# A written order for VectorE, ScalarE, GpSimd and the loads up to the second product, in a fused retention and SiLU kernel

## The chip, the cores and the metric

The kernel runs on one core of a Trainium2 chip. TensorE (PE in the profile; PEld is its weight load) multiplies into PSUM, VectorE (DVE) and ScalarE (ACT) work elementwise, GpSimd (POOL) makes constants, and SyncE (SP) issues DMAs between HBM and SBUF. The metric is the device time of one execution in microseconds (us), as a median over runs; lower is better.

## The reference

Two parts follow each other. Retention: for 4 batches and 8 heads, over 768 positions with head size 64, a 64x64 state decays and takes up the outer product of k and v, and q reads it. Then a feed-forward part on the 3072 x 512 result.

```python
gamma = 1.0 - 2.0 ** (-5.0 - np.arange(H))
for t in range(S):
    state = gamma[None, :, None, None] * state + np.einsum('bhd,bhe->bhde', k[:, :, t], v[:, :, t])
    y[:, :, t] = scale * np.einsum('bhd,bhde->bhe', q[:, :, t], state)
x = y.transpose(0, 2, 1, 3).reshape(B * S, H * D)
h = x @ w_in                      # 512 -> 2048
g = h * (1.0 / (1.0 + np.exp(-h)))
out = g @ w_out                   # 2048 -> 512
```

q, k and v are 32-bit floats. `w_in` and `w_out` arrive as 64-bit floats and are converted on the chip. All three products are made at about 32-bit accuracy, each from three products of rounded parts.

## The kernel before

**Units.** The sequence is cut into 6 chunks of 128 positions; a chunk of one batch is a *unit*, 24 in all, 0 to 3 being chunk 0 of the four batches, 4 to 7 chunk 1, and so on. A unit loads k, q and v (256 KB each, `load`, L137). The units go through a pipeline of *visits* (`halves`, L544): visit m transposes k and q of unit m (`stage_t`, L396; ScalarE copies them out, L405), makes the sums and scores of unit m-1 (`stage_s` L419, `stage_a` L429) and y of unit m-2 (`stage_y`, L462). VectorE scales k (`scale_k`, L365), masks the scores (am, L437), forms mid and state (L446, L450; mid is a ScalarE copy in chunk 0, L444), scales q (L370) and splits y into three parts of x (`finish_y`, `split_x`: ScalarE L497 and L509, VectorE L512 and L513). From unit 6 on, ScalarE scales k, a head at a time (L354). Between two parts of a unit's y stands a fence, a tiny GpSimd memset (L340).

**Slices of the weights.** `w_in` is used in 16 slices of 128 columns. A slice's 64-bit words are loaded by three DMAs (`load_w`, L170 and L172, 512 KB), converted by one ScalarE operation and six of VectorE (`convert_w`, L198 to L215), and split into three parts by two ScalarE and two VectorE operations (`split_w`, L121 to L126). `take_w` does a whole slice; `begin_w` and `end_w` do it in two visits.

**Products.** `product_in(c, f)` (L592) multiplies chunk c's x by slice f: 8 matmuls into bank ha, 4 into hb (L596). The first four need the rounded high parts, the next four the second parts, and hb the third ones. ScalarE copies ha out (L600), VectorE subtracts hb (L604), ScalarE applies SiLU (L608), and `put_g` stores g to HBM. Product (c, f) needs all four units of chunk c and slice f. The products of chunks 0 to 2 run among the visits; those of later chunks follow. After all g is stored, chunk by chunk, g is loaded back, split (L651 to L654) and multiplied by `w_out` (L761) into pairs of accumulators oa and ob for four batches, which are evacuated (L769 and L770; in the last chunk L773 and L778) and stored.

**What sets the order.** TensorE's order is the program's (`manual_schedule`, L663). That of the other engines and of SP's queue is chosen by the framework's scheduler when the kernel is built; the kernel steers it only with `issue_after`, which puts instructions behind a given one of the same engine. On a queue or engine an instruction that waits holds up what is behind it. Before TensorE's schedule starts, all loads of units 0 to 7 are issued, with slice 0 after unit 1 and slice 1 after unit 4:

```python
    for n in range(EARLY):            # EARLY = 8
        for name in "kqv":
            load(name, n)
        if n in (1, 4):
            load_w(n // 4)
```

The visits then run as follows: product (0, 0) after visit 6, (0, 1) after visit 8, (0, 2) in the middle of visit 9, and (1, 0) after the first half of visit 10.

```python
    for m in range(EARLY + 1):
        visit(m)
        if m == 2:
            take_w()
        elif m == EARLY - 2:
            product_in(0, 0)
            load_w(3)
        elif m == EARLY:
            product_in(0, 1)
            put_g(1)
```

Of the kernel before, what the change touches and what calls it, by code (L numbers as in the profile page):

```python
# [15 lines left out]
U32 = mybir.dt.uint32  # L16
# [17 lines left out]
def kernel(  # L34
# [79 lines left out]
    def split_w(f, w32, name, factor, to, behind_x=False):  # L114


        to[f] = w = w_slot(f, name)
        lo = conv.tile([128, 512], FP32, tag="wl", name=f"{name}l_{f}")
        yield
        with tc.issue_after(held[0] if behind_x or f >= NF - 4 else evac[0]):  # L120
            nc.scalar.activation(out=w[:, 0, :], in_=w32, func=AF.Copy, scale=HALF * factor)  # L121
        high = w[:, 0, :].bitcast(FP32)
        nc.vector.scalar_tensor_tensor(out=lo, in0=w32, scalar=factor, in1=high,
                                       op0=ALU.mult, op1=ALU.subtract)
        nc.scalar.activation(out=w[:, 1, :], in_=lo, func=AF.Copy, scale=1.0 / EPS)
        nc.vector.scalar_tensor_tensor(out=w[:, 2, :], in0=high, scalar=EPS, in1=lo,  # L126
                                       op0=ALU.mult, op1=ALU.subtract)

# [48 lines left out]
    def convert_w(i):  # L177

        if i + W_AHEAD not in staged and i != 1:
            load_w(i + W_AHEAD)
        t = staged.pop(i)
        if not wide:  # L190
            return lambda: t
        words = t.rearrange("p (c w) -> p c w", w=2)
        lo, hi = words[:, :, 0], words[:, :, 1]
        a = conv.tile([128, DM], U32, tag="ca", name=f"ca_{i}")
        s = conv.tile([128, DM], U32, tag="cs", name=f"cs_{i}")
        p = conv.tile([128, DM], U32, tag="cp", name=f"cp_{i}")
        with tc.issue_after(evac[0]) if evac else ExitStack():
            nc.scalar.activation(out=a.bitcast(FP32), in_=hi.bitcast(FP32), func=AF.Abs,  # L198
                                 scale=65536.0)
        nc.vector.tensor_scalar(out=s, in0=hi, scalar1=0x80000000, scalar2=None,  # L200
                                op0=ALU.bitwise_and)
        nc.vector.tensor_scalar(out=a.bitcast(FP32), in0=a.bitcast(FP32),
                                scalar1=bits(1024 << 20), scalar2=bits((1279 << 20) - 1),
                                op0=ALU.max, op1=ALU.min)
        nc.vector.scalar_tensor_tensor(out=s, in0=a, scalar=3, in1=s,  # L205
                                       op0=ALU.logical_shift_left, op1=ALU.bitwise_or)
        nc.vector.tensor_scalar(out=p, in0=s, scalar1=0xFF800000, scalar2=None,
                                op0=ALU.bitwise_and)
        nc.vector.scalar_tensor_tensor(out=p.bitcast(FP32), in0=lo, scalar=2.0 ** -52,  # L209
                                       in1=p.bitcast(FP32), op0=ALU.mult, op1=ALU.mult)  # L210

        def rounded():
            w = (s.bitcast(FP32) if i < NF else
                 conv.tile([128, DM], FP32, tag="wl", name=f"cw_{i}"))
            nc.vector.tensor_tensor(out=w, in0=s.bitcast(FP32), in1=p.bitcast(FP32), op=ALU.add)  # L215
            return w

        return rounded

# [39 lines left out]
    for n in range(EARLY):  # L259
        for name in "kqv":  # L260
            load(name, n)
        if n in (1, 4):
            load_w(n // 4)
# [24 lines left out]
    def chunk_decays():  # L288
        pos = step[:, HP + H :]
        nc.gpsimd.iota(pos, pattern=[[0, 1]], base=1, channel_multiplier=1,  # L290
                       allow_small_or_imprecise_dtypes=True)
        for h in range(H):
            nc.scalar.activation(out=gk[:, 0, h : h + 1], in_=pos, func=AF.Exp,
                                 scale=float(-lg[h]))
            nc.gpsimd.memset(step[:, HP + h : HP + h + 1], math.exp(-C * lg[h]))
            part = ts(h % 2, D)
            nc.gpsimd.memset(step[part, h // 2 : h // 2 + 1], math.exp(C * lg[h]))
            nc.gpsimd.memset(lgc[part, h // 2 : h // 2 + 1], lg[h])
        for c in range(1, NC):
            nc.gpsimd.tensor_tensor(out=gk[:, c, :], in0=gk[:, c - 1, :],  # L300
                                    in1=step[:, HP : HP + H], op=ALU.mult)

    def first_chunk():
        nc.gpsimd.iota(lag, pattern=[[1, C]], base=1, channel_multiplier=0,
                       allow_small_or_imprecise_dtypes=True)
        for a in range(HP):
            nc.scalar.activation(out=gq[:, a, :], in_=lag, func=AF.Exp, scale=lgc[:, a : a + 1])

        nc.scalar.activation(out=token, in_=lgc[:1, :1], func=AF.Silu)
# [123 lines left out]
    def finish_a(n, sc, sums):  # L433

        c, b = units[n]
        am[n] = one.tile([128, 2, HP, D], FP32, tag="am", name=f"am_{n}")
        mask = nc.vector.tensor_tensor(out=am[n], in0=sc, in1=decay, op=ALU.mult).ins  # L437
        masked[:] = [mask]
        mid = one.tile([128, HP, D], FP32, tag="mid", name=f"mid_{n}", bufs=2)
        steps_of[n] = state.get(b), mid  # L440

        with tc.issue_after(mask):
            if c == 0:
                nc.scalar.copy(out=mid, in_=sums[:, 0])  # L444
            else:
                nc.vector.tensor_tensor(out=mid, in0=state[b], in1=sums[:, 0], op=ALU.add)  # L446
            if c < NC - 1:
                state[b] = one.tile([128, HP, D], FP32, tag="state", name=f"state_{n}",
                                    bufs=B + 2)
                nc.vector.tensor_tensor(out=state[b], in0=mid, in1=sums[:, 1], op=ALU.add)  # L450
# [37 lines left out]
    def finish_y(n, yp):  # L488
        c, b = units[n]
        if b == 0:  # L490
            p, tag = (wpool, "wq") if c == LATE else (xpool, "xt")
            xt[c] = p.tile([128, 3, KIN, NT], FP32R, tag=tag, name=f"xt_{c}")
        raw = None
        if c <= LATE:

            raw = hpool.tile([128, KIN, C], FP32, tag="hs", name=f"ys_{n}")
            nc.scalar.copy(out=raw.rearrange("p a (o t) -> p o a t", o=2), in_=yp)  # L497
            if c == LATE:
                nc.sync.dma_start(out=y_dram[b], in_=raw)
        split_x(c, b, yp, raw)  # L500

    def split_x(c, b, y, raw):
        x = [xt[c][:, i, :, ts(b, C)] for i in range(3)]
# [7 lines left out]
        def rest():  # L511
            nc.vector.tensor_tensor(out=xl, in0=src, in1=xh.bitcast(FP32), op=ALU.subtract)  # L512
            nc.vector.scalar_tensor_tensor(out=x[2], in0=x[1].bitcast(FP32),  # L513
                                           scalar=-1.0 / EPS, in1=x[0].bitcast(FP32),
                                           op0=ALU.mult, op1=ALU.add)


        if c > LATE or c == LATE and y is not None:
            behind_next.append(rest)
        else:  # L520
            rest()


# [10 lines left out]
    def late_x(b):  # L534
        if b == 0:
            xt[LATE] = xpool.tile([128, 3, KIN, NT], FP32R, tag="xt", name=f"xt_{LATE}")
        with tc.issue_after(copied[0]), tc.issue_after(taken_out[0]):
            split_x(LATE, b, None, y_late.pop(b))
# [5 lines left out]
    def halves(m):  # L544
# [22 lines left out]
        if m == 0:  # L567
            chunk_decays()
            first_chunk()
# [13 lines left out]
        if EARLY - 3 <= m < 3 * B + 2:  # L583
            with tc.issue_after(masked[0]):
                end_w()
                if m not in (EARLY - 2, EARLY):
# [5 lines left out]
    def product_in(c, f):  # L592
        ha, hb = turn(f"ha_{c}_{f}"), turn(f"hb_{c}_{f}")
        for i in range(3):
            for kk in range(KIN):
                nc.tensor.matmul(hb if i == 2 else ha, lhsT=w_sb[f][:, i, ts(kk, 128)],  # L596
                                 rhs=xt[c][:, i, kk, :], start=kk == 0 and i != 1,
                                 stop=kk == KIN - 1 and i != 0)
        hs = hpool.tile([128, NT], FP32, tag="hs", name=f"g_{c}_{f}")
# [63 lines left out]
    ctx.enter_context(tc.manual_schedule(engines={mybir.EngineType.PE}))  # L663


    for m in range(EARLY + 1):
        visit(m)
        if m == 2:
            take_w()
        elif m == EARLY - 2:  # L670
            product_in(0, 0)
            load_w(3)
        elif m == EARLY:
            product_in(0, 1)
            put_g(1)
    half_visits = (x for m in range(EARLY + 1, 3 * B + 1) for x in chain(halves(m), (None,)))
    next(half_visits)
    product_in(0, 2)
    put_g(1)
    next(half_visits)  # L680
# [58 lines left out]
    for c in range(NC):  # L739
        acc = []  # L740
        for b in range(B):
# [3 lines left out]
            else:  # L745
                acc.append([turn(f"oa{b}_{c}"), turn(f"ob{b}_{c}") if b == 2 else
                            banks("q", f"ob{b}_{c}", 1)[:, 0]])
        for f in range(NF):
# [4 lines left out]
            t = ready.pop(n)  # L753
            first_, last = f == 0, f == NF - 1
            for b in range(B):
                gh, glo, gm = (t[:, i, ts(b, C)] for i in range(3))
                oa, ob = acc[b]
                todo = [(oa, gh, 0), (oa, glo, 1), (ob, gm, 2)]

                for o, g, i in todo if c < NC - 1 else todo[2:] + todo[:2]:  # L760
                    nc.tensor.matmul(o, lhsT=g, rhs=wo[f][:, i, :], start=first_ and i != 1,  # L761
                                     stop=last and i != 0)
# [49 lines left out]
```

## Time and profile before

| what | value |
|---|---|
| median of 4 runs | 629.75 us (628.37 to 631.83) |
| the profiled execution's own time | 629.2 us |
| its span, from first to last instruction of the program | 627.4 us |
| mean granted TensorE clock | 0.996 |
| start of product (0, 0) / (0, 1) / (0, 2) / (1, 0) | 37.02 / 50.65 / 55.33 / 61.56 us |
| first work of VectorE | 7.86 us |
| landing of slice 0 / slice 1 / slice 2 | 12.2 / 26.3 / 41.2 us |
| landing of q of unit 7 / unit 8 | 36.6 / 42.8 us |
| first and last matmul of the second matrix product | 359.7 and 622.4 us |

The profile is one execution. Its page gives busy times by engine, 40 slices of the span, DMA queues, the chain of work that ended last, and the costliest groups of instructions. A line of a timeline reads: start, duration, engine, source line, operation, output<-inputs, shape, and in brackets how long the engine had been idle and what ended that. "Issue" means that the engine waited for nothing that the profile shows.

### The profile page before, as it was taken

To read this page: it belongs to the slowest core of one execution; us is meant where nothing else is said; L and a number is where in the kernel's file an instruction comes from. 1 tells how busy PE (TensorE), PEld (TensorE's weight loads), DVE (VectorE), ACT (ScalarE), POOL (GpSimd) and SP (SyncE) were. 2 spreads that over 40 slices of the span, in tenths; PEclk is the share of its full clock that TensorE was granted. 3 is DMA by queue.
4 is the path that set the end of the run, shared out by engine and by line. 5 is a ranking of instruction groups with operands and counts; after the bars stand their busy time and mean duration, and the time that the engine had idled before them with its cause. 6 is when DMAs were issued, how large, how long until landed. Compare 5 with 4: busy or idle time off the path is not lost.

```text
span 627.4 us, 13502 instructions
## 1 busy us (share of the span) xinstructions
PE 603.6 (96%) x5384; PEld 497.0 (79%) x5384; DVE 422.2 (67%) x729; ACT 318.9 (51%) x611; POOL 22.3 (4%) x79
## 2 busy tenths in 40 slices
PE   4778999999999999999999999999999999999997
PEld 3667787888888888888787888888788888888785
DVE  2887998698979876867598795644636453644631
ACT  5688897667665566666466871412222221412211
POOL 3000000000000311111000000000000000000000
PEclk9999999999999999999999999999999999999999
DMA  9987887445559899989566673432523433433301
GB/s 199 212 202 193 214 227 227 160 158 172 202 168 251 208 268 229 262 216 290 195 223 198 217 218 118 140 129 71 178 88 116 154 101 100 142 127 105 97 1 67
DMA packets 137999, 107.32 MB, mean 171 GB/s; under 512 B 94800, under 2 KB 103248, under 8 KB 137936
## 3 DMA queue, kind: packets, MB, share of 16 engines
q1 hardware_dynamic: 135056, 101.21, 57.3%
q10 hardware_dynamic: 2880, 5.24, 2.3%
q8 instruction: 42, 0.69, 0.5%
q14 instruction: 21, 0.17, 0.1%
HBM read 66.06 MB, written 36.70 MB: 164 GB/s over the span
## 4 chain that ended last, share of the span: by engine, by line
PE 88%; DVE 4%; DMA 3%; issue 2%; SPq 2%; ACT 1%; DVEq 0%; ACTq 0%; POOLq 0%
PE ha L596 26%; PE o L761 21%; PE oa L761 14%; PE hb L596 13%; PE ob L761 7%; PE y L462 4%; PE sc L419 2%; PE sc L429 2%; SPq L150 1%; PE qp L403 1%; PE kp L403 1%; DMA kqv<-in_q_dram 1%; DMA wf<-in_moe_w_out_dram 1%; DMA gr<-gd 1%; DMA gd<-g 1%
## 5 line engine op out<-in xcount | busy, mean ns | idle before, releaser
L596 PE MATMUL ha<-xt,wi 128*128 128x512 f32 x768 | 193.1, 393 | 0.8 <-DVE g L604 0.8
L596 PEld LDWEIGHTS ha<-xt,wi 128*128 128x128 f32 x768 | 142.1, 188 | 32.3 <-DVE g L604 2.0
L761 PE MATMUL o<-wo,gs 128*128 128x512 f32 x576 | 146.3, 389 | 0.0
L761 PEld LDWEIGHTS o<-wo,gs 128*128 128x128 f32 x576 | 108.1, 188 | 22.5
L653 DVE TENSOR_TENSOR gs<-gr,gs 128x512 fp32r<-128x512 f32 x96 | 62.3, 685 | 85.3 <-ACT gs L651 85.3
L651 ACT ACTIVATE gs<-gr 128x512 fp32r<-128x512 f32 x96 | 53.5, 621 | 127.9 <-issue 123.6
L761 PE MATMUL oa<-wo,gs 128*128 128x512 f32 x384 | 118.4, 389 | 0.0
L596 PE MATMUL hb<-xt,wi 128*128 128x512 f32 x384 | 103.0, 390 | 0.2 <-ACT g L600 0.2
L604 DVE TENSOR_TENSOR g<-g,hb 128x512 f32<-128x512 f32 x96 | 65.6, 683 | 47.2 <-ACT g L600 34.3
L596 PEld LDWEIGHTS hb<-xt,wi 128*128 128x128 f32 x384 | 71.8, 188 | 16.0 <-ACT g L600 1.2
L761 PEld LDWEIGHTS oa<-wo,gs 128*128 128x128 f32 x384 | 72.0, 188 | 15.3 <-ACT o L769 0.3
L608 ACT ACTIVATE g<-g 128x512 f32<-128x512 f32 x96 | 60.5, 631 | 44.0 <-DVE g L604 43.9
L761 PE MATMUL ob<-wo,gs 128*128 128x512 f32 x192 | 75.3, 392 | 0.3 <-DVE o L770 0.3
L600 ACT ACTIVATE g<-ha 128x512 f32<-128x512 f32 x96 | 56.9, 592 | 29.2 <-PE ha L596 20.2
L654 DVE SCALAR_TENSOR_TENSOR gs<-gs 128x512 fp32r<-128x512 f32 x96 | 62.2, 684 | 0.1
L761 PEld LDWEIGHTS ob<-wo,gs 128*128 128x128 f32 x192 | 36.0, 188 | 9.4 <-DVE o L770 2.1
L198 ACT ACTIVATE ca<-wf 128x512 f32<-128x512 f32 x32 | 21.6, 674 | 10.1 <-DVE cs L205 5.8
L209 DVE SCALAR_TENSOR_TENSOR cp<-wf,cp 128x512 f32<-128x512 uint32 x32 | 22.7, 711 | 0.6
L769 ACT ACTIVATE o<-o 128x512 f32<-128x512 f32 x10 | 6.0, 600 | 33.4 <-PE o L761 33.0
L205 DVE SCALAR_TENSOR_TENSOR cs<-ca,cs 128x512 uint32<-128x512 uint32 x32 | 22.1, 690 | 0.8
L462 PE MATMUL y<-qt,mid 64*64 64x64 f32 x384 | 20.4, 221 | 0.0
L770 DVE TENSOR_TENSOR o<-o,o 128x512 f32<-128x512 f32 x10 | 6.8, 688 | 19.3 <-ACT o L769 19.3
(85 smaller groups left out, 566.9 us busy)
## 6 DMA issues: line engine op xcount, KB each, us to landing
gd<-g SPq DMA_DIRECT2D x96, 256.0 KB, 3.3
gr<-gd SPq DMA_DIRECT2D x96, 256.0 KB, 2.7
wf<-in_moe_w_out_dram SPq DMA_DIRECT2D x16, 512.0 KB, 4.3
out_dram<-o ACTq DMA_DIRECT2D x20, 256.0 KB, 2.1
wf<-in_moe_w_in_dram SPq DMA_DIRECT2D x16, 256.0 KB, 4.2
wf<-in_moe_w_in_dram SPq DMA_DIRECT2D x32, 128.0 KB, 4.0
kf<-in_k_dram SPq DMA_DIRECT2D x16, 256.0 KB, 5.3
qf<-in_q_dram SPq DMA_DIRECT2D x16, 256.0 KB, 4.4
```

Source lines behind the costliest of these rows:

```text
L198: nc.scalar.activation(out=a.bitcast(FP32), in_=hi.bitcast(FP32), func=AF.Abs, scale=65536.0)
L205: nc.vector.scalar_tensor_tensor(out=s, in0=a, scalar=3, in1=s, op0=ALU.logical_shift_left, op1=ALU.bitwise_or)
L209: nc.vector.scalar_tensor_tensor(out=p.bitcast(FP32), in0=lo, scalar=2.0 ** -52, in1=p.bitcast(FP32), op0=ALU.mult, op1=ALU.mult)
L462: i = nc.tensor.matmul(yp[ts(e, D), o, a, :], lhsT=lhsT, rhs=rhs, start=(e, o) not in started, stop=True, skip_group_check=True).ins
L596: nc.tensor.matmul(hb if i == 2 else ha, lhsT=w_sb[f][:, i, ts(kk, 128)], rhs=xt[c][:, i, kk, :], start=kk == 0 and i != 1, stop=kk == KIN ...
L600: copied[:] = [nc.scalar.activation(out=hs, in_=ha, func=AF.Copy, scale=ONE_E).ins]
L604: taken_out[:] = [nc.vector.tensor_tensor(out=hs, in0=hs, in1=hb, op=ALU.subtract).ins]
L608: nc.scalar.activation(out=hs, in_=hs, func=AF.Silu)
L651: nc.scalar.activation(out=t[:, 0, :], in_=g, func=AF.Copy, scale=HALF)
L653: nc.vector.tensor_tensor(out=t[:, 1, :], in0=g, in1=high, op=ALU.subtract)
L654: nc.vector.scalar_tensor_tensor(out=t[:, 2, :], in0=t[:, 1, :].bitcast(FP32), scalar=-1.0 / EPS, in1=high, op0=ALU.mult, op1=ALU.add)
L761: nc.tensor.matmul(o, lhsT=g, rhs=wo[f][:, i, :], start=first_ and i != 1, stop=last and i != 0)
```

## The change

Up to the second product the order of VectorE, ScalarE, GpSimd and SP is written down as well. The helpers become generators whose steps are single instructions (`convert_steps`, `split_steps`, `steps_a`, `steps_y`), and a list of calls puts them in order: T transposes a unit, K scales its k, SC makes sums and scores, A is one step of am, mid and state, Q scales q, YA and YB are the two parts of y, X one step of copying out and splitting y, W one step of a slice.

- Loads: units 0 to 5 are issued at the start, slice 0 after unit 0, slice 1 after unit 3; then slice 2, units 6 and 7, slice 3.
- Product (0, 0) stands after the transposes of unit 4 and (0, 1) after those of unit 5, then visits 6 and 7, (0, 2) in the middle of visit 8, visit 9 and the first half of visit 10. From product (1, 0) on, TensorE's order is as before.
- Slices 2 and 3 begin in visits 6 and 8 (before: 7 and 9).
- The constants are made in a written order; the memsets of `step` come after what the first unit needs.
- A conversion keeps ca and cp in one buffer, and `w_out`'s converted slices have a buffer of their own.
- In the second matrix product every chunk takes oa before ob in a step (the last chunk began with ob). In the last chunk the last two steps are taken batch by batch: ob for both, then oa for both, so that the batches finish one after the other.

```diff
-    for n in range(EARLY):
+    ctx.enter_context(tc.manual_schedule(engines={mybir.EngineType.PE}))
+    early_order = ExitStack()
+    early_order.enter_context(tc.manual_schedule(engines={
+        mybir.EngineType.SP, mybir.EngineType.DVE, mybir.EngineType.Activation,
+        mybir.EngineType.Pool}))
+    for n in range(EARLY - 2):
         for name in "kqv":
             load(name, n)
-        if n in (1, 4):
-            load_w(n // 4)
+        if n in (0, 3):
+            load_w(n // 3)
...
-        a = conv.tile([128, DM], U32, tag="ca", name=f"ca_{i}")
+        p = a = conv.tile([128, DM], U32, tag="ca", name=f"ca_{i}")
...
+    def early_slice(i):
+        out = []
+        yield from convert_steps(i, out)
+        yield
+        steps = split_steps(i, out[0], "wi", scale, w_sb, None)
+        next(steps)
+        yield from steps
...
-        if EARLY - 3 <= m < 3 * B + 2:
+        if EARLY - 2 <= m < 3 * B + 2:
             with tc.issue_after(masked[0]):
                 end_w()
-                if m not in (EARLY - 2, EARLY):
+                if m not in (EARLY - 1, EARLY + 1):
                     begin_w()
...
+    T(0), K(0)
+    nc.scalar.activation(out=token, in_=lgc[:1, :1], func=AF.Silu)
+    SC(0), A(0), Q(0), A(0), A(0)
+    W(0), W(0), W(0), W(0), W(0)
+    YA(0), YB(0), X(0)
+    T(1), K(1)
+    W(0)
+    load_w(2)
+    W(0)
+    X(0), X(0)
+    SC(1), A(1)
...
+    YA(3), YB(3), X(3), X(3)
+    W(1)
+    T(4), K(4)
+    X(3), X(3)
+    W(1), W(1), W(1)
+    loads(EARLY - 2), loads(EARLY - 1)
+    first_of = multiply(0, 0)
+    next_chunk()
+    SC(4)
+    close_in(0, 0, *first_of)
+    put_g(1)
+    W(1)
+    A(4)
+    W(1), W(1)
+    A(4), A(4), Q(4)
+    W(1), W(1)
+    T(5), K(5)
+    taken[0] = 2
+    load_w(3)
+    early_order.close()
+
+    product_in(0, 1)
+    put_g(1)
+    visit(EARLY - 2)
+    visit(EARLY - 1)
+    eighth = halves(EARLY)
+    next(eighth)
     product_in(0, 2)
     put_g(1)
-    next(half_visits)
+    list(eighth)
+    visit(EARLY + 1)
+    half_visits = (x for m in range(EARLY + 2, 3 * B + 1) for x in chain(halves(m), (None,)))
     next(half_visits)
...
-                todo = [(oa, gh, 0), (oa, glo, 1), (ob, gm, 2)]
-
-                for o, g, i in todo if c < NC - 1 else todo[2:] + todo[:2]:
+                for o, g, i in (oa, gh, 0), (oa, glo, 1), (ob, gm, 2):
...
+        for b in range(B if early_f < NF else 0):
+            oa, ob = acc[b]
+            for o, parts in (ob, (2,)), (oa, (0, 1)):
+                for f in range(early_f, NF):
+                    for i in parts:
+                        nc.tensor.matmul(o, lhsT=ready[c * NF + f][:, i, ts(b, C)],
+                                         rhs=wo[f][:, i, :], start=False,
+                                         stop=f == NF - 1 and i != 0)
```

## The prediction

> **What bounds the kernel now.** I read the totals first (the second line is a DMA queue: packets, MB, share), then the table of windows, then the timeline of the first 65 us, and last the chain of waits at the end. The totals:
>
> ```profile
> PE 603.6 (96%) x5384; PEld 497.0 (79%) x5384; DVE 422.2 (67%) x729; ACT 318.9 (51%) x611; POOL 22.3 (4%) x79
> ...
> q8 instruction: 42, 0.69, 0.5%
> ```
>
> TensorE (PE) is idle for 627.4 - 603.6 = 23.8 us of the span. The change adds no matmul and removes none, so it can only move these 23.8 us. The windows say where they lie (columns: PE, PEld, DVE, ACT, POOL busy, granted clock, DMA share, GB/s):
>
> ```profile
> 0.00:10.00 10.00, 4.19 (x16) 2.86 (x16) 1.42 (x2) 6.74 (x24) 4.83 (x41) 1.00 0.95 183
> 10.00:20.00 10.00, 7.62 (x194) 6.50 (x192) 5.25 (x11) 4.15 (x9) 0.16 (x2) 0.83 1.24 215
> 20.00:30.00 10.00, 7.31 (x263) 6.43 (x264) 9.75 (x20) 7.76 (x17) 0.18 (x2) 1.00 0.96 224
> 30.00:40.00 10.00, 7.98 (x239) 7.00 (x239) 8.56 (x17) 7.76 (x21) 0.29 (x2) 1.00 0.88 199
> 40.00:50.00 10.00, 6.21 (x270) 5.43 (x268) 9.15 (x19) 8.93 (x26) 0.43 (x2) 1.00 0.82 187
> 50.00:60.00 10.00, 9.61 (x167) 7.93 (x168) 6.65 (x12) 8.20 (x20) 0.09 (x1) 1.00 0.69 184
> 60.00:70.00 10.00, 9.56 (x160) 7.58 (x159) 9.30 (x20) 8.10 (x21) 0.09 (x1) 1.00 0.84 196
> 70.00:80.00 10.00, 10.00 (x177) 8.21 (x178) 9.60 (x19) 8.94 (x24) 0.09 (x1) 1.00 0.96 249
> 90.00:100.00 10.00, 9.38 (x99) 7.32 (x92) 9.93 (x20) 9.02 (x23) 0.00 (x0) 1.00 0.88 238
> ```
>
> In the first 50 us PE is idle for 5.8 + 2.4 + 2.7 + 2.0 + 3.8 = 16.7 us; from 50 to 100 us for 1.5 us; the end after the last matmul has most of the rest. So the head is what the change can win. But there VectorE (DVE) is busy for 27.5 of the 30 us from 20 to 50 and stays above 9.3 of 10 to 100 us, and the DMA share is 0.82 or more. Three resources are near their limit together. What the idle stretches wait for:
>
> ```profile
> 30.77 0.35 PE L462 MATMUL y<-am,kqv 64*64 64x64 f32 x9 [1.59 <-issue]
> ...
> 35.37 0.27 PE L462 MATMUL y<-am,kqv 64*64 64x64 f32 x2 [1.25 <-issue]
> ...
> 45.85 0.44 PE L403 MATMUL qp<-ident,qf 128*128 128x128 f32 x2 [2.10 <-issue]
> ...
> 50.39 0.27 PE L462 MATMUL y<-qt,state 64*64 64x64 f32 x1 [2.07 <-issue]
> ...
> 58.57 0.69 DVE L604 TENSOR_TENSOR g<-g,hb 128x512 f32<-128x512 f32 x1 [3.11 <-ACT g L600]
> ```
>
> Four times PE waits for nothing in the program, 7.0 us together. Counted along PE's and PEld's records these places are numbers 961, 1217, 1729 and 1985: always a multiple of 256 apart. The totals agree: 5384 + 5384 instructions over 42 fetches is 256 each. So PE is waiting for its own instructions: the resumption at 30.77 is 5.1 us after the one at 25.68 (number 705), 35.37 is 4.6 later, 50.39 is 4.5 after 45.85. I take 4.8 us for every 256 PE instructions while the DMA is this full.
>
> **The change, part by part.** *Constants.* GpSimd's selects now stand ahead of the memsets, so `decay` need not wait for 4.01 and gk is ready near 4.4. The first scaling of k (7.86 before, released by gk) then follows its transpose's end at 5.43: 5.5. What this is worth is part of the walk below.
>
> *Loads.* Slice 0 goes ahead of unit 1, slice 1 ahead of unit 4, slice 2 ahead of unit 6. Before, the DMAs of a unit land 1.2 us apart, a slice's three take 1.03 + 0.56 + 0.49. So slice 0 lands at 6.60 + 2.1 = 8.7 (12.2 before), unit 1's v at 12.2 (10.1), unit 3's v stays at 20.4 and slice 1 lands near 22.5 (26.3). Queued behind them on SP: units 6 and 7 by about 37 and 40, slice 3, the first store of g, and only then k and q of unit 8, after 9.17 MB instead of 8.39.
>
> *VectorE's order, walked.* Ready 512-wide operations start 0.60 apart, 256-wide ones 0.33, dependent ones 0.71. am of unit 0 starts at 8.4 (sums after v at 6.6, then scores 0.75), w0's add at 13.3, am of unit 1 at 14.5, w0's last split at 17.8, am of unit 2 at 18.35, of unit 3 at 22.2, k of unit 4 at 26.2, then the last two x pieces: 28.2. Product (0,0) starts at about 26.2 (37.0 before) and ends at 29.5. Then eleven VectorE operations for g, slice 1 and unit 4 end w1's last split at 34.6; product (0,1) ends at 35.7 (53.7 before).
>
> This is 18 us earlier, and hardly any of it is a gain: by then PE has done some 1150 instructions (16 for a unit's transposes, 128 for its scores, 96 or 128 for its y, 24 for a product), where the records before count 2017. The orders meet again at product (1,0), 61.56 before, whose hb part at 63.51 needs the last x piece of unit 7. What VectorE does from 35.1 to there: one g (0.6), four units' am, mid, q, state (7.5), four x pairs (4.8), slice 2 (4.2), slice 3 up to its first split (3.6), another g (0.6) = 21.3, where 0.5 more goes to dependent steps. Its idle: 0.6 for product (0,1)'s end; 2.55 while PE does unit 6's transposes, y of unit 4 and the scores of unit 5; 0.85 behind ScalarE's thirteen operations (k of unit 6 alone costs 2.02, as before); 1.55 because product (0,2) waits for slice 2's last split and the next am stands behind it; 0.35 for the scores of unit 7: 5.9. The sum is 35.1 + 21.3 + 0.5 + 5.9 = 62.8, against 63.51: **-0.7**. The cause is that slice 3 now converts ahead of (1,0), 3.0 us of work that was partly behind it. I take -0.55, as ends are later by pipeline latency.
>
> PE's fetch pace allows no more than 2.9 us: number 1217 falls in y of unit 4 at 37.4, four more blocks give 56.6 for number 2241, the rest to (1,0) and its ha part bring hb to 60.6.
>
> In the Trainium skill, "Runtime: NRT & Kernel Launch", section "Instruction fetch mechanics", instruction memory is refilled in blocks of 256 instructions and the cost of crossing a boundary is called mostly hidden. The block size agrees with the rows here, the hiding does not (1.25 to 2.10 us each). By the page the 7.0 us would be removable by order alone and the sum below would be that much lower; by the rows they are a pace, and I go by the rows.
>
> *After (1,0).* PE has no gap to 96.8, so VectorE's lead (1.2 us of slice 3's splits plus about 1.7) buys only the waits of PE for VectorE at 97.44 (0.62) and 100.78 (0.17): between 0 and -0.8; **-0.4**, the middle, as DMA stores also stand in that chain.
>
> *Own buffers of the conversions.* One buffer serves ca and cp, another cw: a later slice's first step waits for the earlier one's add. Takes are at least two products (5.4 us) apart, which hides it; uncovered it would cost one 0.71.
>
> *Last chunk's order.* Chunk 5 began with ob, held by VectorE's evacuation. In the chain of waits a switch to chunk 4 takes 2.88 for a step of 2.72, the one to chunk 5 8.79 for three steps (8.16):
>
> ```profile
> 534.91 1.36 PE o L761 x6
> 537.79 1.39 PE o L761 x6
> ...
> 573.18 1.36 PE o L761 x6
> 581.97 1.37 PE o L761 x6
> ```
>
> With oa first it is like the others: 0.63 - 0.16 = **-0.45**. At the end the accumulators now finish 1.36 apart instead of 0.68, so the third one's 0.68 on VectorE is out of the way of the last two halves, which today start 0.5 after the last matmul's end at 622.78, and three of the five stores have left: **-0.45**, between -0.2 and -0.7.
>
> Sum: -0.55 - 0.4 - 0.45 - 0.45 = -1.85 us; span 627.4 -> 625.55. The profiled execution took 629.2 (1.8 around its span); the median of four is 629.75, so 629.75 - 1.85 = **627.9 us**.
>
> **Rivals.** *A, only the fetch pace holds the head.* If VectorE's 5.9 us of idle are mostly filled, hb starts at 60.6: -2.9 - 0.4 - 0.9 = -4.2, 625.5 us. For it: PE's four issue waits. Against: VectorE above 9 tenths.
>
> *B, the loads become the bound (slower).* k and q of unit 8 are behind 0.79 MB more. In the walk PE asks for them at 44 to 45.2. At the early pace (8.39 MB by 42.8) q lands at 46.8; then product (0,2)'s hb moves from 50.85 to 52.0 and (1,0)'s by the same 1.15. From a landing at 47.5 on the head's gain and the tail's are used up, as each microsecond is one of the product. Landing gaps of 3.0 us (32.9 to 35.9 before) show that 50 is possible: +4.3 by the loads - 1.85 = +2.45, 632.2 us. Against: SP issues far ahead.
>
> *C, nothing moves.* The head is even and only the tail stays: -0.9, 628.85.
>
> **How the numbers follow.** Forecast 0.45, A 0.27, B 0.15, C 0.13. A change of 0.5% (3.15 us, about what a measurement can tell) divides at 626.6 and 632.9. A lies beyond 626.6 in most of its cases (0.23), the forecast in few (0.06): faster 0.29. B lies beyond 632.9 in half of its cases, the others hardly: slower 0.10. Same 0.61. The range goes down to A with the shortest block seen, 4.5 for 4.8 (four blocks, 1.2 more): 629.75 - 2.9 - 1.2 - 0.8 - 1.15 (the tail at best) = 623.7, and up to B's 632.2. The likeliest case's own is 626.4 to 629.4.
>
> **What would show it.** Product (0,0) near 26, (0,1) ending near 36, slice 0's first VectorE step at 9 to 10; "issue" waits still on PE at numbers 1473 and 1729; VectorE nearly full from 42 to 63; (1,0) at 60 to 61.5; a PE step of 2.9 at chunk 5. Wrong if (1,0) starts before 58 (VectorE was not the limit) or after 63 with PE waiting for a load of unit 8 or 9.

## The result, and the profile after

| what | before | after |
|---|---|---|
| median | 629.14 us (74 runs) | 630.96 us (48 runs) |
| ratio, with 95% interval | | 1.0036 [1.0026, 1.0046] |
| the profiled execution's time / span | 629.2 / 627.4 us | 630.3 / 628.3 us |
| start of product (0, 0) / (0, 1) | 37.02 / 50.65 us | 28.70 / 33.84 us |
| start of (0, 2) / (1, 0) | 55.33 / 61.56 us | 49.52 / 62.80 us |
| first and last matmul of the second product | 359.74 / 622.39 us | 361.38 / 624.26 us |

The changed kernel is 0.36% slower, about 2.3 us, where 1.85 us less was forecast. The time lies inside the range given, the sign is wrong.

The first line of the page's totals (the DMA line has the same 42 fetches as before):

```profile
PE 605.5 (96%) x5384; PEld 497.7 (79%) x5384; DVE 423.1 (67%) x729; ACT 318.8 (51%) x611; POOL 22.6 (4%) x79
```

PE's idle time is 628.3 - 605.5 = 22.8 us, 1.0 *less* than before. Its busy time rose by 1.9 us with the same 5384 matmuls. So the idle time alone doesn't show where the time went: matmuls that take longer count as busy. Next, PE's rows in the head with an idle time in brackets (start, duration, ..., idle before and what ended it):

```profile
21.38 0.68 PE L493 MATMUL y<-am,kqv 64*64 64x64 f32 x26 [0.80 <-ACT ys L531]
22.48 0.34 PE L493 MATMUL y<-am,kqv 64*64 64x64 f32 x6 [0.42 <-issue]
25.70 0.69 PE L493 MATMUL y<-am,kqv 64*64 64x64 f32 x32 [1.54 <-ACT ys L531]
...
42.53 0.69 PE L493 MATMUL y<-am,kqv 64*64 64x64 f32 x32 [0.85 <-ACT ys L531]
...
46.30 0.27 PE L493 MATMUL y<-qt,state 64*64 64x64 f32 x1 [1.68 <-issue]
```

```profile
49.12 0.27 PE L493 MATMUL y<-qt,state 64*64 64x64 f32 x1 [0.75 <-DVE qt L395]
...
51.32 1.20 PE L637 MATMUL ha<-xt,wi 128*128 128x512 f32 x4 [0.61 <-ACT wi L127]
...
58.20 0.50 PE L454 MATMUL sc<-qt,kt 64*64 64x64 f32 x17 [0.68 <-issue]
...
60.97 0.69 PE L493 MATMUL y<-am,vf 64*64 64x64 f32 x32 [0.94 <-DVE am L462]
62.41 0.27 PE L493 MATMUL y<-qt,state 64*64 64x64 f32 x1 [0.75 <-DVE qt L395]
```

In these two profiles the waits for instructions fell from 7.0 us to 2.8. Waits for ScalarE and VectorE took their place: three for ScalarE's copy of y (ys), one for a split of slice 2, one for q of unit 6, two for am and q of unit 8.

The second place is in the middle, where `w_out` is converted while chunk 5 is multiplied. ScalarE, PE and VectorE in the changed kernel:

```profile
328.84 0.58 ACT L644 ACTIVATE g<-ha 128x512 f32<-128x512 f32 x1
...
330.43 0.63 ACT L121 ACTIVATE wo<-wr 128x512 fp32r<-128x512 f32 x1 [1.01 <-DMA wr<-wod]
...
331.82 0.63 ACT L127 ACTIVATE wo<-wol 128x512 fp32r<-128x512 f32 x1 [0.76 <-DVE wol L124]
332.36 0.58 ACT L644 ACTIVATE g<-ha 128x512 f32<-128x512 f32 x1
333.24 0.68 DVE L648 TENSOR_TENSOR g<-g,hb 128x512 f32<-128x512 f32 x1
...
333.98 1.21 PE L637 MATMUL ha<-xt,wi 128*128 128x512 f32 x4 [1.71 <-DVE g L648]
```

ScalarE has two split steps of `w_out` ahead of the copy of ha, with nothing between them. The first waits 1.01 for its slice from HBM, the second 0.76 for VectorE. The copy, 0.54 behind them, is late, so VectorE's subtraction is, and PE waits 1.71 us for the bank. Before, PE had 0.52 us of idle time from 300 to 370 us, now 2.44.

The third place is the end. The chain of waits at the switch to chunk 5 and at the last matmuls (start, time on the chain, engine, what):

```profile
580.95 1.36 PE o L886 x6
582.99 0.46 PE oa L886 x2
583.83 1.38 PE o L886 x6
...
622.38 0.91 PE oa L894 x4
623.75 0.92 PE oa L894 x4
```

The switch is a step of 583.83 - 580.95 = 2.88 as forecast, without a stop. From the start of the last matmul to the end of the span it is 4.04 us, where it was 5.02.

### The profile page after: what moved, and what is told of

Same layout as the page of the kernel before. It is cut to its first block, busy times and chain, and to the rows that moved or that the text cites. A ratio compares the mean times of both kernels' runs of the same rounds, so it can differ in the third digit from the quotient of the medians.

```text
span 628.3 us, 13488 instructions
## 1 busy us (share of the span) xinstructions
PE 605.5 (96%) x5384; PEld 497.7 (79%) x5384; DVE 423.1 (67%) x729; ACT 318.8 (51%) x611; POOL 22.6 (4%) x79
## 5 line engine op out<-in xcount | busy, mean ns | idle before, releaser
L886 PE MATMUL o<-wo,gs 128*128 128x512 f32 x564 | 143.2, 389 | 0.0
L886 PEld LDWEIGHTS o<-wo,gs 128*128 128x128 f32 x564 | 105.9, 188 | 21.9
L886 PE MATMUL oa<-wo,gs 128*128 128x512 f32 x376 | 115.9, 389 | 0.3 <-DVE g L648 0.3
L886 PEld LDWEIGHTS oa<-wo,gs 128*128 128x128 f32 x376 | 70.5, 188 | 15.3 <-DVE g L648 0.7
L886 PE MATMUL ob<-wo,gs 128*128 128x512 f32 x188 | 73.8, 393 | 0.1
L462 DVE TENSOR_TENSOR am<-sc,decay 128x512 f32<-128x512 f32 x24 | 16.5, 688 | 10.2 <-PE sc L454 10.1
L213 DVE SCALAR_TENSOR_TENSOR ca<-wf,ca 128x512 f32<-128x512 uint32 x32 | 22.7, 709 | 0.4
```

The costliest lines, as they stand in the source:

```text
L886: nc.tensor.matmul(o, lhsT=g, rhs=wo[f][:, i, :], start=f == 0 and i != 1, stop=f == NF - 1 and i != 0)
```

## The experiments

"Old buffers" means the old kernel's separate ca and cp, and cw in the split's buffer. Each ratio is to the kernel before on the same chip. The first four part the change in three. Theory 1 in their expectations is that the three parts add up: head and buffers cost, the tail gives.

**e1, the tail alone**: the kernel before with the new loops of the second product.

> The kernel of before with the new order of the second matrix product alone. Theory 1 (three parts of the change add up: head slower, shared conversion buffers slower, new order of the second product faster): faster by 1.0 to 1.5 us (0.45 to 0.6 at the last switch of chunks, 0.5 to 1.0 behind the last matmul), some 627.9 us against 629.1. Rival (the changed kernel's later matmul end is what shortens its tail, not the order): no difference, within 0.3 us.

627.28 us, ratio 0.9973 [0.9954, 0.9992]. From first to last matmul of the second product 262.14 us (262.65 before), from there to the end 4.03 (5.02): -1.5 by the trace, -1.7 by the ratio. The tail is worth more than forecast.

**e2, the buffers alone**:

```diff
-        a = conv.tile([128, DM], U32, tag="ca", name=f"ca_{i}")
+        p = a = conv.tile([128, DM], U32, tag="ca", name=f"ca_{i}")
-        p = conv.tile([128, DM], U32, tag="cp", name=f"cp_{i}")
-                 conv.tile([128, DM], FP32, tag="wl", name=f"cw_{i}"))
+                 conv.tile([128, DM], FP32, tag="cw", name=f"cw_{i}"))
```

> The kernel of before with only the conversion's buffers changed (ca and cp are one buffer, cw has its own). Theory 1: slower by 1.5 to 2.2 us, with a wait of ScalarE's first conversion step for the add of the slice ahead and a TensorE gap of 1 us or more between 325 and 345 us. Rival (the gap at 332 us in the changed kernel is a matter of that execution or of the shifted head): no difference, within 0.3 us.

629.12 us, ratio 1.0008 [0.9992, 1.0024]. The trace has stops of 0.67 us at 330.38 and 0.34 at 361.28 that before doesn't have: 1.1 us of idle time more from 300 to 370 us. The time alone couldn't show that: Theory 1 had 1.5 to 2.2 us, and 0.5 with an interval from -0.5 to 1.5 is what was measured.

**e3, the head alone** (old buffers, old tail), and **e4, head and tail** (the changed kernel with old buffers):

> The written order and the new loads and visits alone, with the buffers and the second product of before. Theory 1: slower by 0.5 to 1.2 us, product (1, 0) starting at 62.5 to 63 us, no gap of TensorE over 1 us at 332 us. Rival (the head alone makes the loss): slower by 2.3 us or more.

> The changed kernel with the conversion's buffers of before. Theory 1: 1.5 to 2.2 us faster than the changed kernel, so equal to before or up to 0.5 us faster. Rival (the head alone makes the loss): as slow as the changed kernel, 1.5 us or more over before.

e3: 630.8 us, ratio 1.0020 [1.0003, 1.0036]; in its profile (1, 0) starts at 61.80, ahead of the 62.5 to 63 that were expected. e4: 628.56 us, 0.9997 [0.9983, 1.0011], with no stop near 332 (0.30 us idle from 300 to 370). So the head costs 0.0020 x 629 = 1.3 us, and e4 against e1 says 1.5. The buffers, from e4 to the changed kernel, cost 0.0039 x 629 = 2.5 us. Head and tail add up; the buffers cost more here than alone, though the intervals of the two (e2's -0.5 to 1.5 us, and 0.0039 +- 0.0017) touch.

**e5, only ca and cp share** (the changed kernel, with cw in the split's buffer again), beside **e6, the changed kernel again**:

> The changed head and tail, ca and cp in one buffer, but the converted w_out slices still in the buffer of the split's low part (the changed kernel without cw's own buffer). In the built order, ScalarE's copies of ha and its two split steps of w_out alternate here as before; only with cw's own buffer do two split steps stand ahead of a copy of ha. Theory P (cw's own buffer reorders ScalarE around 325 to 335 us): no PE gap near 332, PE idle from 300 to 370 us at most 0.7 us, and a time like the changed head and tail with old buffers, ratio to before 0.999 to 1.001. Rival Q (the shared ca waits for the add and holds ScalarE): the gap near 332 is there (1 us or more), ratio 1.002 to 1.004. Rival R (neither: the middle costs some other way): no gap but a ratio of 1.002 or more.

> The changed kernel itself, on the same chip as the three others. Ratio to before 1.003 to 1.004, PE gap near 332 of 1.2 us or more. If it comes out at 1.001 or less, the difference to its variants was one of chips or of builds and not of buffers.

e5: 628.03 us, ratio 0.9999 [0.9977, 1.0022], 0.30 us idle from 300 to 370. e6: 630.89 us, 1.0042 [1.0018, 1.0065], 1.31 us idle there, 0.68 of it in one stop at 334 (1.2 or more had been expected). The two differ in nothing but cw's own buffer, and in the order that the scheduler builds from there on; their ratios differ by 0.0043, 2.7 us. ScalarE in e6:

```profile
331.06 0.62 ACT L121 ACTIVATE wo<-wr 128x512 fp32r<-128x512 f32 x1
332.53 0.63 ACT L127 ACTIVATE wo<-wol 128x512 fp32r<-128x512 f32 x1 [0.84 <-DVE wol L124]
333.19 0.60 ACT L644 ACTIVATE g<-ha 128x512 f32<-128x512 f32 x1
```

This is the changed kernel's order without the wait for HBM, and e2 has it too, with the same 0.84. The timeline of e5 at the same place:

```profile
334.65 0.64 ACT L121 ACTIVATE wo<-wr 128x512 fp32r<-128x512 f32 x1 [0.31 <-DMA wr<-wod]
...
335.38 0.63 ACT L652 ACTIVATE g<-g 128x512 f32<-128x512 f32 x1
336.05 0.63 ACT L127 ACTIVATE wo<-wol 128x512 fp32r<-128x512 f32 x1
...
336.58 0.58 ACT L644 ACTIVATE g<-ha 128x512 f32<-128x512 f32 x1
...
337.12 1.07 PE L637 MATMUL ha<-xt,wi 128*128 128x512 f32 x4
```

A split step, SiLU, a split step, the copy: VectorE's part is done while ScalarE works on SiLU, and neither the second split step nor the copy waits. Probably the scheduler could not pull the split ahead while cw shared a buffer with the split's low part. So Theory P holds: with a buffer that removes a wait, the order changed for the worse. That it is the order and not the buffer is read from these rows; no run pinned the order and kept the buffer.

**e7, y's copy first** (on e4):

```diff
-    YA(1), SC(2)
-    A(2), A(2), Q(2), A(2)
-    YB(1), X(1), X(1)
+    YA(1), SC(2), A(2)
+    YB(1), X(1)
+    A(2), Q(2), A(2)
+    X(1)
```

(and the same a unit later)

> The changed head and tail with old buffers, and in the written order ScalarE's copy of y of units 1 and 2 (ys) stands ahead of mid of units 2 and 3. Theory H1 (the one y bank, freed by ys, holds PE in the head): the waits of y for ys at about 21.4, 25.7 us (0.8 and 1.5 us) shrink below 0.5 each, product (0,0) starts 0.8 to 1.5 us earlier than with the changed order (30.2 in a profile that started late, 28.7 in the changed kernel), (1,0) 0.5 to 1.5 us earlier, ratio 0.9975 to 0.999. Rival H2 (VectorE's work up to (1,0) sets it, the waits are absorbed): (0,0) may move, (1,0) moves under 0.4 us, ratio 0.999 to 1.001.

628.94 us, ratio 1.0013 [0.9989, 1.0037]. (0, 0) starts at 27.15, (1, 0) at 62.15. Two of its rows on PE:

```profile
24.03 0.69 PE L494 MATMUL y<-am,kqv 64*64 64x64 f32 x32 [0.74 <-ACT ys L532]
...
45.73 0.27 PE L494 MATMUL y<-qt,state 64*64 64x64 f32 x1 [2.56 <-issue]
```

The wait for ys shrank from 1.54 to 0.74, and the wait for instructions at number 1729 grew from 1.68 to 2.56. The stretch from (0, 1) to (0, 2) took 16.65 us, 15.68 in the changed kernel. The fair neighbour is e3, whose TensorE was as fast in the first 16 us: against it (0, 0) is 0.57 us earlier and (1, 0) 0.35 later. H1's early part is right in kind, and the rows have instruction fetch taking it back. The ratio lies above both ranges that were expected.

**e8, slice 3 later** (on e4; visit 9 in place of 8):

```diff
-                if m not in (EARLY - 1, EARLY + 1):
+                if m not in (EARLY - 1, EARLY):
                     begin_w()
```

> The changed head and tail with old buffers, and slice 3 begins in visit 9 in place of visit 8, so that its conversion stands after unit 7's on VectorE, as before the change. Theory H2 (VectorE's work ahead of product (1,0) sets its start, and slice 3's 3 us are what the change put there): (1,0) starts 1.5 to 3 us earlier (60 to 61.3), ratio 0.996 to 0.998. Rival H1 (PE's waits for y's bank and for its instructions set it): (1,0) moves under 0.5 us, ratio 0.999 to 1.001. Third: (1,0) moves earlier, but (1,1) or (1,2) then wait for slice 3 or for unit 8 and the ratio stays.

627.12 us, ratio 0.9982 [0.9964, 1.0], 0.9 us below e4 but within the intervals of the two. (1, 0) starts at 61.84, later than the 60 to 61.3 that were expected. From (0, 2) to (1, 0) it is 11.74 us, where the changed head takes 13.27 or 13.28 in four profiles (14.73 in e5, at half clock there). The last x piece of unit 7 starts at 62.77 where it started at 63.80. But (1, 1) follows 5.38 us after (1, 0) (4.72 before this edit), so 0.7 of the 1.5 goes back: H2 is right in kind, and the third takes part of it.

**e9, e10, e11, VectorE's idle time filled** (on e4): slice 2's conversion begins right after product (0, 1); e10 has slice 3 in visit 9 too, e11 also y's copy first.

```diff
+    begin_w()
     visit(EARLY - 2)
...
-                end_w()
-                if m not in (EARLY - 1, EARLY + 1):
+                if m > EARLY - 2:
+                    end_w()
+                if m not in (EARLY - 2, EARLY - 1, EARLY + 1):
                     begin_w()
```

> The changed head and tail with old buffers, and slice 2's conversion begins right after product (0,1) in place of visit 6, so that VectorE does it in the 0.8 and 1.9 us in which it waited for the sums and scores of unit 5. In every profile of the changed head so far, with slice 3 in visit 8, product (0,1) to (0,2) took 15.7 to 16.7 us and (0,2) to (1,0) 13.1 to 13.3 (one that waited there 14.7). Theory H2 (VectorE's order sets this stretch): the 28.95 us from (0,1) to (1,0) shrink by 1.5 to 2.5, ratio to before 0.995 to 0.998. Rival F (TensorE's pace of instruction fetch sets it): the time goes into issue waits, the stretch shrinks under 1 us, ratio 0.999 to 1.001.

> The same and slice 3 in visit 9. H2: the two add up, from (0,1) to (1,0) 25 to 26.5 us, ratio 0.993 to 0.997, the best so far. F: like the run with slice 3 later alone (27.4 us), ratio 0.998 to 0.999. Third: (1,0) starts earlier, but (1,1) waits for slice 3's splits, so that (1,1) gains half of it or less.

> The same and y of units 1 and 2 copied ahead of mid of units 2 and 3. If the y bank's waits were a cost that reaches the end, the ratio is 0.0008 to 0.0015 lower than without; if VectorE or instruction fetch takes it back (as the stretch from (0,1) to (0,2) did in the run with this edit alone, 16.65 us against 15.68), it is the same within 0.0005.

All three missed: 630.01, 628.98 and 628.31 us, ratios 1.0046 [1.0022, 1.0069], 1.0016 [1.0004, 1.0028] and 1.0005 [0.9990, 1.0019]. From (0, 1) to (1, 0) they took 31.0, 29.7 and 30.1 us. PE in e10:

```profile
45.29 0.27 PE L494 MATMUL y<-qt,state 64*64 64x64 f32 x1 [1.68 <-issue]
...
48.32 0.99 PE L429 MATMUL kp<-ident,kf 128*128 128x128 f32 x4 [2.69 <-DMA kf<-in_k_dram]
```

VectorE's 0.76 and 1.94 us of idle time were gone, but `begin_w` also issues the load of slice 4, and now ahead of unit 8. In e10 its k landed at 48.27 (44.13 in the changed kernel), and PE waited 2.69 for it, in e11 2.33. In e9, whose PE came later to this place, it waited only 0.59 for k and 0.47 for q. In all three TensorE also stood at half clock in this stretch, in e9 from 49.8 to 56.6 us, in e10 and e11 for 3.4 us from 48.5 and 48.1. The experiment had moved two things.

**e12, the tail again**, beside them:

> The kernel before with the new order of the second product alone, on the same chip as the three above. Ratio 0.997 to 0.998. If the head with VectorE's idle filled is better than the old one, the run with both slice edits comes out below this; if not, the old head with the new tail is the best version.

626.78 us, ratio 0.9977 [0.9965, 0.9990].

**e13, e14, e15, the same three with slice 4's load behind unit 8's k and q**, where the changed kernel has it:

```diff
-        if i + W_AHEAD not in staged:
+        if i + W_AHEAD not in staged and i != 2:
             load_w(i + W_AHEAD)
...
                 if m > EARLY - 2:
                     end_w()
+                else:
+                    load_w(4)
```

> The fill run (slice 2's conversion right after product (0,1), slice 3 in visit 8) with slice 4's load left behind k and q of unit 8, where the changed head has it; before, the fill had moved 0.5 MB ahead of unit 8, k of unit 8 landed at 48.3 in place of 44.1, and TensorE waited 2.7 us for it. Theory L (the loads of unit 8, not VectorE or fetch, took the fill's gain): no wait of TensorE for k or q of unit 8 above 0.7 us, product (0,1) to (1,0) 26.5 to 27.7 us (28.95 in the changed head, about 31 in the fill run), ratio 0.0025 to 0.006 below that of the fill run (1.0046), so 0.9985 to 1.002. Rival F (fetch or ScalarE takes the place): the waits for loads go, but the stretch stays at 28.5 or more, ratio within 0.001 of the changed head and tail (0.9997).

> The same with slice 3 in visit 9. L and VectorE's order together: product (0,1) to (1,0) 25.5 to 26.7 us, ratio 0.995 to 0.998, at or below slice 3 later alone (0.9982). F: like slice 3 later alone, 27.4 us and 0.998 to 0.999.

> The same and y of units 1 and 2 copied ahead of mid of units 2 and 3: product (0,0) 0.5 to 0.7 us earlier at the same rate of TensorE in the first 16 us, the stretch from (0,1) to (1,0) longer by as much if fetch or loads take it back (ratio within 0.0007 of the run without), else ratio 0.0008 to 0.0012 below it.

627.92, 627.25 and 626.22 us; ratios 0.9993 [0.9976, 1.0010], 0.9978 [0.9960, 0.9995], 0.9972 [0.9957, 0.9987]. No wait for a load of unit 8 above 0.4 us is left. By the ratios the three are 0.0053, 0.0038 and 0.0033 below e9 to e11: 0.5 MB ahead of unit 8 cost 2 to 3 us, with all that followed from it. (The 48.3 and 2.7 us in the expectation are e10's.) From (0, 1) to (1, 0) they took 29.46, 27.24 and 26.08 us. The first two lie above what was expected. Both profiles have TensorE at half clock near 48 to 50 us, e13 again at 66, and e15 in neither place, so what the lengths say of fetch against VectorE stays open, and so does e15's gain over e14, which is inside the intervals. With all four edits (1, 0) starts at 59.93, and no cost of the head is left to be seen. But e15 and the tail alone (0.9973 and 0.9977) can't be told apart: both beat both kernels, and the simple one does it with a few lines.

## Why the prediction was wrong, step by step

**The account.** In us, from the ratios (x 629):

| part | forecast | measured |
|---|---|---|
| head and what follows (-0.55 - 0.4) | -0.95 | +1.3 (e3), +1.5 (e4 against e1) |
| tail (-0.45 - 0.45) | -0.9 | -1.7 (e1), -1.45 (e12) |
| buffers | 0 | +2.5 (after against e4), +2.7 (e6 against e5), +0.5 alone (e2) |
| sum | -1.85 | +2.3 (the changed kernel) |

Each measured part has an interval of one to two us on either side (e3 0.2 to 2.3, e1 -2.9 to -0.5). Two steps failed: the buffers, put at nothing, and the head with its base, put at a gain.

**Buffers: wrong, and the largest error.** The step reads "a later slice's first step waits for the earlier one's add. Takes are at least two products (5.4 us) apart, which hides it". It priced the wait that a shared buffer adds, and e5 shows no cost of that (0.9999, e4 0.9997). It did not price the wait that cw's own buffer *removes*, after which the scheduler orders ScalarE anew. The traces see 1.0 to 2.1 us of stops, the times 2.5 with the new head and 0.5 [-0.5, 1.5] alone. Whether the head makes it dearer is not settled.

**The walk of VectorE: right up to 18 us, then two waits were missed.** e3's profile, in which TensorE had its full rate early, against the forecast of 13.3 (w0's add), 14.5 (am of unit 1), 18.35 and 22.2 (am of units 2 and 3):

```profile
13.28 0.69 DVE L219 TENSOR_TENSOR cs<-cs,cp 128x512 f32<-128x512 f32 x1
14.49 0.68 DVE L463 TENSOR_TENSOR am<-sc,decay 128x512 f32<-128x512 f32 x1
...
18.36 0.68 DVE L463 TENSOR_TENSOR am<-sc,decay 128x512 f32<-128x512 f32 x1
...
21.81 0.69 PE L445 MATMUL sc<-kqv 64*64 64x64 f32 x32 [0.70 <-DMA kqv<-in_v_dram]
...
23.04 0.69 DVE L463 TENSOR_TENSOR am<-sc,decay 128x512 f32<-128x512 f32 x1 [0.99 <-PE sc L455]
```

Three times exact, then 0.84 late, and 0.80 late at the end: hb of (1, 0) is at 63.76, forecast 62.96. The exactness is partly luck: five of the thirteen profiles with the new head are as fast this early, and in the other eight am of unit 1 starts at 15.7 to 15.9.

The first thing missed is a load. The sums of unit 3 wait 0.70 us for its v, which landed at 21.68 in e3, where the forecast has "20.4". The second is that y has one PSUM bank. PE can't begin y of unit 2 until ScalarE has copied y of unit 1, and in the written order that copy stands behind mid of unit 2, which by the trace waits for am. The rows with "ACT ys" above are this wait. In e6, e8, e13 and e14, where no load holds unit 3, am of unit 3 follows am of unit 2 by 4.02 us, forecast 3.85; with y copied first it follows by 3.44 and 3.53 (e11, e15), and (0, 0) starts 0.7 to 0.8 us earlier in e15 than in e13 and e14. So the bank is a cost, but most of e3's 0.84 is the load. A walk that follows one engine must look at loads, and at what the other engines' order does to shared banks.

A reading was wrong too. VectorE "stays above 9.3 of 10 to 100 us" passes over the window from 50 to 60 us in the same table, where VectorE is busy for 6.65 and the DMA share is 0.69.

**The base of the sum: one late execution.** I set 62.96 against the 63.51 of the profile before. In e1 and e2, the old head in other executions, the same hb starts at 62.40 and 62.75. Against these, 63.76 is a loss of 1.0 to 1.4 us, not a gain of 0.55, and that agrees with the 1.3 of e3's ratio. The drop of TensorE's clock from 10 to 20 us in the profile before (0.83 in the windows) is not what made it late: product (0, 0) starts at 37.02 there and at 36.91 and 36.97 in e1 and e2. From there to (0, 1) it takes 13.62 us, 12.36 in e1, 12.91 in e2. The waits for instructions in that stretch are 2.10 and 2.07 us before, and in e1 and then e2:

```profile
44.74 0.44 PE L403 MATMUL qp<-ident,qf 128*128 128x128 f32 x2 [1.10 <-issue]
...
49.01 0.27 PE L462 MATMUL y<-qt,state 64*64 64x64 f32 x1 [1.45 <-issue]
```

```profile
45.08 0.44 PE L402 MATMUL qp<-ident,qf 128*128 128x128 f32 x2 [1.36 <-issue]
...
49.62 0.27 PE L461 MATMUL y<-qt,state 64*64 64x64 f32 x1 [2.00 <-issue]
```

So these waits vary by up to a microsecond each with the same head. (The median of four, 629.75, was high as well: of 74 it is 629.14.) e12, the old head once more, has 63.76, with TensorE at half clock from 49.1 to 52.5 us.

**Left out of the sum: the clock.** Of the 170 executions with the old head whose granted clock is on record (before, e1, e2, e12) 4 have a mean of 0.992 or less, of the 193 with the new head 58, 18 of them among 49 of the changed kernel. In e6 the four such executions average 633.2 us and the other eight 630.2, where before has 628.6 above 0.992 on the same chip. So about 0.9 of e6's 2.6 us comes with the lower clock and 1.7 without it. The difference of 2.6 us between e5 and e6 is the same above 0.992 (627.6 and 630.2). What in the new order brings the lower clock no run shows.

**What follows (1, 0): right in size.** Forecast -0.4. (1, 0) is 1.24 us later than before, the 21st product (123.39, before 122.67) only 0.72: -0.5. Against e1 it would be -0.4, against e2 -0.1.

**Tail: right in kind, the end mis-sized.** The switch to chunk 5 was forecast at -0.45 and the trace of e1 has -0.5. The end was forecast at -0.45, between -0.2 and -0.7, and it measured 5.02 - 4.03 = -1.0. I had counted one operation of VectorE and the stores as gone; staggering the accumulators brought twice that. (The step at the switch is 0.47 by its own numbers, 0.63 - 0.16.)

**What was to show it.** Slice 0's first VectorE step came at 10.19 (9 to 10 expected), (0, 0) at 28.70 (26), the end of (0, 1) at 37.75 (36). VectorE is busy for 18.0 of the 21 us from 42 to 63, not nearly full. Of the issue waits, 1729 is there (46.30), 1473 is not; 2241 is. (1, 0) came at 62.80, outside 60 to 61.5. The step of 2.9 at chunk 5 is there (2.88).

**The rivals.** B gave the loads of unit 8 as the slower case. Its q landed at 46.29 (B had 46.8), just in time: TensorE has no stop for a load above 0.5 us in the changed kernel's head. e10 shows the price that B named from 47.5 on: k at 48.27, 2.69 us. A, the fetch pace, is what took e7's gain. So three limits lie close to each other in this stretch, as the prediction said, and freeing one shows the next. The one slower case was B, by the loads of unit 8. Neither the reordered ScalarE nor the lower clock was among the rivals, nor a base that was one late execution.

## What to carry to other kernels

Where a scheduler builds the order, a buffer edit is an order edit. Compare the built order of every engine around the buffer's users, and look for a waiting step that now stands ahead of a copy which frees a bank. A sum against one profile takes over the waits of that execution: take a second one, and compare the granted clocks of all executions. And where several limits lie close together, move one thing at a time: e9 to e11 hid their own gain behind a load that came along with the edit.

## What the runs showed of the hardware

TensorE's rate in the first 16 us differs from execution to execution with the same head. Transposes of units 1 and 2, in e3 and then in the changed kernel:

```profile
10.98 0.66 PE L429 MATMUL kp<-ident,kqv 128*128 128x128 f32 x4
...
13.79 0.66 PE L429 MATMUL kp<-ident,kqv 128*128 128x128 f32 x4
```

```profile
11.93 1.11 PE L428 MATMUL kp<-ident,kqv 128*128 128x128 f32 x4
...
15.74 0.87 PE L428 MATMUL kp<-ident,kqv 128*128 128x128 f32 x4
```

Four transposes take 0.66 or 1.11 us, though the granted clock reads 1.00 in both. The changed kernel's profile reaches the fast rate at least 5 us later, and is 1.0 us later at (0, 0) and at (1, 0). Later the clock drops: in eight of the thirteen profiles with the new head somewhere from 22 to 33 us, in some of them or the others again from 46 to 57 or from 64 to 71 us. In e4 (columns: PE, PEld, DVE, ACT, POOL busy, granted clock, DMA share, GB/s):

```profile
22.00:24.00 2.00, 1.61 (x60) 1.64 (x64) 0.00 (x0) 0.00 (x0) 0.00 (x0) 0.50 0.63 148
...
26.00:28.00 2.00, 1.64 (x42) 1.45 (x44) 1.57 (x3) 1.22 (x3) 0.09 (x1) 0.50 1.19 258
...
30.00:32.00 2.00, 2.00 (x7) 1.63 (x6) 1.97 (x4) 1.84 (x6) 0.00 (x0) 0.50 1.15 229
```

Half clock for some 10 us: e4's (1, 0) starts at 65.14, e3's at 61.80. This is a second reason why one profile of a head is not a base to a microsecond. In e7, e10, e11, e13 and e14 the half clock sets in within 0.7 us of the end of a wait of 2.3 to 2.7 us. But the profile before has waits of 2.10 and 2.07 us, at 45.85 and 50.39, with the granted clock at 1.00 around them, so the length of a wait alone doesn't settle it. The Trainium skill, "TensorE: Matmul & The Clock Gate", section "What's actually happening", says that TensorE runs at half clock until it has been busy for about 3.4 us, in a window that runs free, so that the point varies by run. The two starts agree with that. It also says that the half clock returns after an idle window of that length. The rows don't show such a window: the longest idle time of TensorE from 8 to 22 us in e4 is 1.26 us.
